# Summary merges and factors with a PSUM operand, and a new order table

## The chip, the cores and the metric

The kernel runs on one core of a Trainium2 chip. The metric is the device time of one execution in microseconds (us). Three executions of the kernel before took 1714.06, 1714.22 and 1714.65 us; the median is 1714.22 us.

## The reference

Two stages follow each other. In the first, 32 inducing vectors `I` (32 x 128) attend to a batch `x` of 12480 rows of 128 values, for each of four batches, which gives a summary `h` of 32 x 128; then every row of `x` attends to that summary. In the second, all 49920 rows go through a two-layer network with a piecewise activation.

```python
def mab(q, kv):
    s = scale * (q @ kv.transpose(0, 2, 1))
    s = s - s.max(-1, keepdims=True)
    a = np.exp(s)
    a /= a.sum(-1, keepdims=True) + 1e-09
    return a @ kv
h = mab(I, x)
attn = mab(x, h)
...
h = x @ w_in
g = np.where(h >= 1, h, np.where(h <= -1, 0.0, (h + 1) ** 2 / 4))
out = g @ w_out
```

## The kernel before

The 12480 rows of a batch are cut into 25 chunks (20 of 512 rows, 5 of 448; `SIZES`), and the chunks into seven groups (`GROUPS`: six of four chunks, the last with one). Three kinds of work are interleaved on all engines:

- **The network (`chunk`, from line 1482 on).** A chunk takes eight steps `k` over the 2048 hidden columns, two halves of 128 each. TensorE (PE) makes the hidden values into two PSUM banks (`hidden`, L1530). ScalarE (ACT) writes `relu(0.5 h + 0.5)` to the buffer `w` (`rise`, L1538) and squares it (L1524). VectorE (DVE) combines `max(h, 1)` from the bank with `w` (`bound`, L1543). For six of the eight steps `w` is then split into a rounded part `hi` (L1573 on DVE, L1571 on ACT or L1567 on GpSimd, POOL) and the rest `lo = w - hi`, which is always POOL's (L1578). PE multiplies by the second weights into an accumulator bank (`project`, L1606). At a chunk's end DVE transposes the accumulator (`oT`, L1618) and SyncE (SP) stores it. `rise` and `bound` take both halves in one instruction ("wide", 128x1024 or 128x2x448) where the order says so and the two banks lie beside each other, otherwise one half each.
- **The summary (`summarize`).** For each group, scores, their maximum, exponentials (`e`, with their sums in a column of `sg`), and the weighted sum of the rows, which `keep` (L1174) puts into `hs[:, g, :]` (128 x 128). A chain of small steps `c1` to `c13` joins the groups when the maxima of the first six are there. `c6` makes the six factors `fe` (ACT, L1221). `c7` makes `fs = fe * sg` and sums it to `early` (DVE, L1224 and L1225). `merge(g)` adds `hs[g] * fe[g]` into `he`, one group after the other (DVE, L1229 for the first, L1231 for the other five). `c8` makes `fall` (ACT, L1234), `c9` makes `tot = early * fall + sg` (DVE, L1237), `c10` folds it on PE (L1240). `c11` makes `rs` and its reciprocal and from them two scaled copies `ff` of the 128 x 32 matrix `fold` (DVE, L1243 to L1246). `c12` multiplies `he` and the last `hs` by `ff` (PE, L1250), and `c13` copies the result to `hT` (DVE, L1254). Everything that reads the next batch's summary waits for `hT`: `multiply` and the loads of `hw`, and the scores of `attend`. Batch 0's summary stands at the start, where no network work runs; those of batches 1 to 3 are interleaved with the network work of the batch before.
- **The attention (`attend`)** of each group against `hT`, with its rows sent to the buffers `aT` by DMA.

Every step is added to a `Plan` with an engine, two costs and its needs. `ORDER` gives each step its rank on its engine, `ON` picks the engine where a step has a choice, and `Plan.order` walks these lists and gives out banks and buffers. An engine works strictly in its order. The plan treats a step marked `alone` on DVE as one that can't run beside POOL. PSUM has eight banks, seven of them (`h=7`) for hidden values, scores and the chain, one (`o=1`) for the accumulator. Each of `s_m`, `s_b`, `s_t`, `s_h` in the chain holds one of the seven for a while. PE runs small products (`keep_on`, L1634) at the start where it would else be idle.

```python
def merge(g):
    if g == 0:
        nc.vector.tensor_scalar(he, hs[:, 0, :], fe[:, :1], None, op0=ALU.mult)
        return
    nc.vector.scalar_tensor_tensor(he, hs[:, g, :], fe[:, g : g + 1], he, op0=ALU.mult, op1=ALU.add)
```

Of the kernel before, what the change touches and what calls it, by code (L numbers as in the profile page):

```python
# [13 lines left out]
ALU = mybir.AluOpType  # L14
# [718 lines left out]
def attn_moe(  # L733
# [276 lines left out]
    def summarize(b):  # L1010
# [184 lines left out]
        tot = small("tot", [P, 1], f"_{b}")  # L1195
        rs = small("rs", [P, 1], f"_{b}")
        ff = small("ff", [P, 2, M], "")
        s_m, s_b, s_t, s_h = (Slot("h") for _ in range(4))

        def c1():  # L1200
            nc.vector.tensor_reduce(m1, mg[:, : NG - 1], axis=AX.X, op=ALU.max)
# [488 lines left out]
```

## Time and profile before

| what | value |
|---|---|
| median of three executions | 1714.22 us |
| the profiled execution, its own time | 1713.46 us |
| its span, first to last instruction | 1711.7 us |
| PE busy | 1683.9 us, 98% |
| DVE busy | 1640.0 us, 96% |
| ACT busy | 1648.2 us, 96% |
| POOL busy | 1610.4 us, 94% |
| mean granted TensorE clock | 0.999 |
| DMA | 105.65 MB, 62 GB/s |

A group of the profile is one line's instructions on one engine, with busy time, mean duration, and the idle time of the engine just before them with what ended it. An instruction that is held up after it has been issued shows this as a longer duration, not as idle time. Matmuls overlap, so PE's busy time is more than its work.

### The profile page before, as it was taken

Reading aid. Unit: us, or ns where it says so; the run is one execution under the profiler, and the core shown is the slowest. Engines: PE = TensorE matmul, PEld = TensorE weight load, DVE = VectorE, ACT = ScalarE, POOL = GpSimd, SP = SyncE. Lnnn points to the kernel's source line nnn. Section 1 sums busy time; section 2 is a strip of 40 time slices with the busy share of each in tenths; the row PEclk is TensorE's granted clock in tenths of the full one; section 3 lists DMA queues with packets and bytes.
Section 4 is the critical chain, followed back from the end, with each engine's and each line's share of the span. In section 5 each row is a group of like instructions: output and inputs, shape, how many; then the busy total and the mean of one; then the engine's idle time right before and its main releaser. Section 6 shows DMA issues by size and latency. Waiting matters only on the chain.

```text
span 1711.7 us, 24841 instructions
## 1 busy us (share of the span) xinstructions
PE 1683.9 (98%) x7713; PEld 1188.8 (69%) x7713; DVE 1640.0 (96%) x2040; ACT 1648.2 (96%) x2220; POOL 1610.4 (94%) x849
## 2 busy tenths in 40 slices
PE   9999999999999999999999999999999999999998
PEld 7766766767667666766766676677667766666677
DVE  7899999999999999999999999999999999999997
ACT  5999999999899999999999999999989999999997
POOL 2799999999899999999899999999989999999998
PEclk9999999999999999999999999999999999999999
DMA  6542323322333241432152432422213112011111
GB/s 250 134 92 41 81 60 68 70 48 54 76 67 70 55 86 39 80 58 56 29 108 52 85 71 49 85 50 41 42 24 66 27 31 42 19 37 42 26 32 26
DMA packets 426212, 105.65 MB, mean 62 GB/s; under 512 B 369744, under 2 KB 409776, under 8 KB 426080
## 3 DMA queue, kind: packets, MB, share of 16 engines
q1 hardware_dynamic: 424960, 103.74, 28.3%
q8 instruction: 61, 1.00, 0.2%
q14 instruction: 71, 0.58, 0.1%
q10 hardware_dynamic: 1120, 0.33, 0.1%
HBM read 48.94 MB, written 25.56 MB: 44 GB/s over the span
## 4 chain that ended last, share of the span: by engine, by line
PE 86%; DVE 7%; ACT 2%; issue 2%; DMA 1%; SPq 1%; POOL 0%; DVEq 0%; ACTq 0%; POOLq 0%
PE banks L1606 61%; PE banks L1530 19%; DVE w L1543 3%; PE banks L1167 1%; PE banks L1338 1%; PE banks L1098 1%; DVE hi L1573 1%; ACT w L1524 1%; ACT w L1538 1%; DVE oT L1618 1%; PE banks L1634 1%; PE banks L1044 1%; PE banks L1148 1%; DMA xr<-in_x 1%; DVE he L1231 0%
## 5 line engine op out<-in xcount | busy, mean ns | idle before, releaser
L1578 POOL TENSOR_TENSOR lo<-w,hi 128x1024 fp32r<-128x1024 f32 (+1 forms) x597 | 1388.3, 2355 | 41.7 <-PE banks L1606 16.3
L1543 DVE SCALAR_TENSOR_TENSOR w<-banks,w 128x1024 f32<-128x1024 f32 (+3 forms) x1098 | 950.8, 902 | 22.4 <-ACT w L1524 15.7
L1538 ACT ACTIVATE w<-banks 128x512 f32<-128x512 f32 (+3 forms) x1162 | 815.9, 753 | 22.6 <-PE banks L1530 17.1
L1524 ACT ACTIVATE w<-w 128x1024 f32<-128x1024 f32 (+1 forms) x800 | 819.5, 1052 | 5.8
L1530 PE MATMUL banks<-aT,hw 128*128 128x512 f32 (+1 forms) x1600 | 601.7, 432 | 12.4 <-DVE w L1543 10.0
L1606 PE MATMUL banks<-hi,w_lo 128*128 128x512 f32 (+1 forms) x1194 | 507.1, 425 | 4.1 <-DVE oT L1618 3.1
L1573 DVE TENSOR_REDUCE hi<-w 128x1024 fp32r<-128x1024 f32 (+1 forms) x391 | 459.5, 1180 | 11.5 <-PE banks L1606 2.9
L1606 PE MATMUL banks<-hi,w_hi 128*128 128x512 f32 (+1 forms) x1194 | 462.3, 387 | 0.0
L1606 PE MATMUL banks<-lo,w_hi 128*128 128x512 f32 (+1 forms) x1194 | 457.1, 430 | 1.9 <-DVE oT L1618 1.3
L1530 PEld LDWEIGHTS banks<-aT,hw 128*128 128x128 f32 x1600 | 296.7, 188 | 165.4 <-DVE w L1543 58.6
L1606 PE MATMUL banks<-w,w_f 128*128 128x512 f32 (+1 forms) x812 | 404.0, 582 | 0.1
L1606 PEld LDWEIGHTS banks<-hi,w_lo 128*128 128x128 f32 x1194 | 224.9, 188 | 103.2 <-issue 43.8
L1606 PEld LDWEIGHTS banks<-lo,w_hi 128*128 128x128 f32 x1194 | 223.6, 188 | 101.4 <-issue 54.3
L1606 PEld LDWEIGHTS banks<-hi,w_hi 128*128 128x128 f32 x1194 | 224.9, 188 | 59.4 <-issue 22.0
L1606 PEld LDWEIGHTS banks<-w,w_f 128*128 128x128 f32 x812 | 151.8, 188 | 38.7 <-issue 10.6
L1567 POOL TENSOR_SCALAR hi<-w 128x1024 fp32r<-128x1024 f32 (+1 forms) x140 | 144.6, 1035 | 8.4 <-DVE w L1543 5.1
L1618 DVE STREAM_TRANSPOSE oT<-banks 128x512 f32<-128x512 f32 (+1 forms) x100 | 69.8, 698 | 10.7 <-PE banks L1606 8.6
L1571 ACT CAST hi<-w 128x1024 fp32r<-128x1024 f32 (+1 forms) x66 | 67.7, 1026 | 0.5 <-DVE w L1543 0.4
L1074 DVE STREAM_TRANSPOSE xT<-xr 128x512 f32<-128x512 f32 (+1 forms) x75 | 51.3, 684 | 4.8 <-DMA xr<-in_x 4.1
L1381 POOL TENSOR_TENSOR a<-a,ahi 128x512 fp32r<-128x512 f32 (+3 forms) x28 | 35.3, 1260 | 0.0
L1370 POOL TENSOR_TENSOR s<-s,sm 128x512 f32<-128x512 f32 (+3 forms) x28 | 28.8, 1030 | 1.3 <-DVE sm L1367 0.8
L1098 PE MATMUL banks<-xT,indT 128*32 128x512 f32 (+1 forms) x224 | 29.0, 589 | 0.0
(130 smaller groups left out, 532.8 us busy)
## 6 DMA issues: line engine op xcount, KB each, us to landing
out<-oT SPq DMA_DIRECT2D x320, 64.0 KB, 2.1
xn<-in_x SPq DMA_DIRECT2D x64, 256.0 KB, 3.3
xr<-in_x SPq DMA_DIRECT2D x240, 64.0 KB, 2.5
aT<-ahi SPq DMA_DIRECT2D x158, 64.0 KB, 2.0
aT<-a SPq DMA_DIRECT2D x158, 64.0 KB, 2.0
xn<-in_x SPq DMA_DIRECT2D x20, 224.0 KB, 3.1
out<-oT SPq DMA_DIRECT2D x78, 56.0 KB, 1.9
xr<-in_x SPq DMA_DIRECT2D x60, 56.0 KB, 2.2
```

The source lines that it names most:

```text
L1074: nc.vector.transpose(make(xT[b, c])[:, : CW[c]], xr.tile[:, : NB[c]].rearrange("c n i -> c (n i)"))
L1098: nc.tensor.matmul(p[q * M : (q + 1) * M, :cw], indT, xT[b, c].tile[:, :cw], start=True, stop=True)
L1524: nc.scalar.activation(v, v, AF.Square)
L1530: nc.tensor.matmul(make(h)[:, :cw], hw[b][ft // 4].tile[:, ft % 4 * P : (ft % 4 + 1) * P], aT[b, c].tile[:, :cw], start=True, stop=True,)
L1538: each(of, i, hs_, lambda h, to: nc.scalar.activation(to, h, AF.Relu, bias=0.5, scale=0.5), cw, w)
L1543: lambda h, t: nc.vector.scalar_tensor_tensor(t, h, 1.0, t, op0=ALU.max, op1=ALU.min), cw, w,
L1567: nc.gpsimd.tensor_scalar(make(hi)[:, :, :cw], w.tile[:, :, :cw], 1.0, 0.0, op0=ALU.mult, op1=ALU.add)
L1571: nc.scalar.copy(make(hi)[:, :, :cw], w.tile[:, :, :cw])
L1573: nc.vector.tensor_reduce(make(hi)[:, :, :cw], w.tile[:, :, :cw].unsqueeze(3), axis=AX.X, op=ALU.max)
L1578: nc.gpsimd.tensor_sub(make(lo)[:, :, :cw], w.tile[:, :, :cw], hi.tile[:, :, :cw].bitcast(F32))
L1606: nc.tensor.matmul(acc.tile[:, :cw], wt[k][:, i, :], g.tile[:, i, :cw], start=first, stop=(acc.parts == 0),)
L1618: nc.vector.transpose(make(oT)[:, :nb].rearrange("c n i -> c (n i)"), acc.tile[:, :cw])
```

## The change

In the four summaries, one more PSUM bank `s_e` is taken from `c6` to the last merge. `c6` writes the factors twice, into columns 128 to 133 of that bank and to `fe`. `c7` reads the copy in the bank. The first merge goes to ACT and writes to the bank; four merges read and write the bank, the last reads the bank and writes `he` to SBUF. `c9` goes from DVE to ACT. In `c11` the reciprocal is written to the bank of `s_t`, and both `ff` read it there as a broadcast operand. `merge` is no longer marked `alone`, and some costs of the plan change. All of `ORDER` is new (of the table two lines stand here), and 28 of the 705 letters of `ON`, which decide engines.

```diff
 ORDER = [
-    0, 0, 2, 0, 4, 0, 2, -2, -2, -2, -2, -2, -2, -2, -2, -2, -2, -2, -2, -2, -2, -2, -2, -2,
+    0, 2, 0, 0, 4, 6, 6, -2, -2, -2, -2, -2, -2, -2, -2, -2, -2, -2, -2, -2, -2, -2, -2, -2,
...
-        s_m, s_b, s_t, s_h = (Slot("h") for _ in range(4))
+        s_m, s_b, s_e, s_t, s_h = (Slot("h") for _ in range(5))
...
         def c6():
-            nc.scalar.activation(fe, mg[:, : NG - 1], AF.Exp, bias=nm, scale=SCALE)
+            for p in (make(s_e)[:, C : C + NG - 1], fe):
+                nc.scalar.activation(p, mg[:, : NG - 1], AF.Exp, bias=nm, scale=SCALE)
 
         def c7():
-            nc.vector.tensor_mul(fs, fe, sg[:, : NG - 1])
+            nc.vector.tensor_mul(fs, s_e.tile[:, C : C + NG - 1], sg[:, : NG - 1])
             nc.vector.tensor_reduce(early, fs, axis=AX.X, op=ALU.add)
 
         def merge(g):
             if g == 0:
-                nc.vector.tensor_scalar(he, hs[:, 0, :], fe[:, :1], None, op0=ALU.mult)
+                nc.scalar.mul(s_e.tile[:, :C], hs[:, 0, :], fe[:, :1])
                 return
-            nc.vector.scalar_tensor_tensor(he, hs[:, g, :], fe[:, g : g + 1], he, op0=ALU.mult, op1=ALU.add)
+            nc.vector.scalar_tensor_tensor(
+                he if g == NG - 2 else s_e.tile[:, :C], hs[:, g, :], fe[:, g : g + 1], s_e.tile[:, :C],
+                op0=ALU.mult, op1=ALU.add,
+            )
...
         def c9():
-            nc.vector.scalar_tensor_tensor(tot, early, fall, sg[:, NG - 1 :], op0=ALU.mult, op1=ALU.add)
+            nc.scalar.activation(tot, early, AF.Identity, bias=sg[:, NG - 1 :], scale=fall)
...
         def c11():
             nc.vector.tensor_scalar(rs, s_t.tile[:, :1], 1e-9, None, op0=ALU.add)
-            nc.vector.reciprocal(rs, rs)
-            nc.vector.tensor_scalar(ff[:, 0, :], fold[:, 0, :], fall, rs, op0=ALU.mult, op1=ALU.mult)
-            nc.vector.tensor_scalar(ff[:, 1, :], fold[:, 0, :], rs, None, op0=ALU.mult)
+            nc.vector.reciprocal(s_t.tile[:, 1:2], rs)
+            r = s_t.tile[:, 1:2].to_broadcast([P, M])
+            nc.vector.scalar_tensor_tensor(ff[:, 0, :], r, fall, fold[:, 0, :], op0=ALU.mult, op1=ALU.mult)
+            nc.vector.tensor_mul(ff[:, 1, :], r, fold[:, 0, :])
...
-                factors = add("ACT", 100, 250, c6, [o])
+                factors = add("ACT", 200, 350, c6, [o], [s_e])
...
-        e = add("DVE", 220, 350, c7, [factors, *summed[:-1]])
+        e = add("DVE", 220, 350, c7, [factors, *summed[:-1]], [s_e])
         for g in range(NG - 1):
-            o = add("DVE", 190, 320, lambda g=g: merge(g), [o if g else state.get("chain"), factors, lasts[g]], alone=g > 0)
+            o = add(
+                "DVE" if g else "ACT", 240 if g else 170, 370 if g else 310, lambda g=g: merge(g),
+                [o if g else state.get("chain"), factors, lasts[g]], [s_e],
+            )
...
-        o = add("DVE", 90, 220, c9, [o, e, summed[-1]])
+        o = add("ACT", 100, 250, c9, [o, e, summed[-1]])
         o = add("PE", 120, 300, c10, [o], [s_t])
-        o = add("DVE", 420, 560, c11, [o, fell, state.get("chain")], [s_t])
+        o = add("DVE", 440, 580, c11, [o, fell, state.get("chain")], [s_t])
```

The order of the instructions moves as follows at the summary of batch 1; batches 2 and 3 look alike. On DVE before, at the end of the chain (`tot` is `c9`; `w` and `hi` are the network's; line numbers are those of the kernel before):

```order
L1237 SCALAR_TENSOR_TENSOR tot_134<-early_132,fall_133,sg 128x1
L1618 STREAM_TRANSPOSE oT_4368<-banks 128x448
L1243 TENSOR_SCALAR rs_135<-banks 128x1
L1244 RECIPROCAL rs_135<-rs_135 128x1
L1245 TENSOR_SCALAR ff<-fold,fall_133,rs_135 128x32
L1246 TENSOR_SCALAR ff<-fold,rs_135 128x32
L1543 SCALAR_TENSOR_TENSOR w_4335<-banks,w_4335 128x448
```

On DVE now, the rows that lead up to the same point (line numbers are eight higher there for the network's lines):

```order
L1232 SCALAR_TENSOR_TENSOR banks<-hs,fe_130,banks 128x128
L1551 SCALAR_TENSOR_TENSOR w_4249<-banks,w_4249 128x448
L1232 SCALAR_TENSOR_TENSOR banks<-hs,fe_130,banks 128x128
L1225 TENSOR_TENSOR fs_131<-banks,sg 128x6
L1226 TENSOR_REDUCE early_132<-fs_131 128x1
L1232 SCALAR_TENSOR_TENSOR banks<-hs,fe_130,banks 128x128
L1551 SCALAR_TENSOR_TENSOR w_4257<-banks,w_4257 128x2x448
L1232 SCALAR_TENSOR_TENSOR banks<-hs,fe_130,banks 128x128
L1551 SCALAR_TENSOR_TENSOR w_4276<-banks,w_4276 128x448
L1232 SCALAR_TENSOR_TENSOR he<-hs,fe_130,banks 128x128
L1626 STREAM_TRANSPOSE oT_4326<-banks 128x448
L1247 TENSOR_SCALAR rs_135<-banks 128x1
```

Before, the six merges of batch 1 stood up to 64 rows ahead of `rs` (rows 432 to 468 of DVE's order, `rs` being row 496); now the five that DVE keeps stand in rows 485 to 494, `rs` being row 496 again. On ACT before, at the same place (`fall` is `c8`):

```order
L1538 ACTIVATE w_4335<-banks 128x2x448
L1123 ACTIVATE e_1171_4342,sg<-banks,nb_6_143 32x448
L1234 ACTIVATE fall_133<-mb_128,nb_6_143 128x1
L1524 ACTIVATE w_4335<-w_4335 128x2x448
L1538 ACTIVATE w_4358<-banks 128x2x448
```

On ACT now:

```order
L1222 ACTIVATE banks<-mg,nm_127 128x6
L1222 ACTIVATE fe_130<-mg,nm_127 128x6
L1546 ACTIVATE w_4276<-banks 128x448
L1230 ACTIVATE banks<-hs,fe_130 128x128
L1238 ACTIVATE fall_133<-mb_128,nb_6_143 128x1
L1532 ACTIVATE w_4257<-w_4257 128x2x448
L1546 ACTIVATE w_4276<-banks 128x448
L1123 ACTIVATE e_1172_4296,sg<-banks,nb_6_143 32x448
L1532 ACTIVATE w_4276<-w_4276 128x2x448
L1241 ACTIVATE tot_134<-early_132,sg,fall_133 128x1
```

The factors, which stood 66 rows ahead of `fall`, now stand four rows ahead of it, and the first merge and `tot` have come in between the network's instructions. Over the whole program, 53 more of ACT's `rise` and 52 more of DVE's `bound` are wide (`rise` of 128x1024: 402 against 349; `bound` of 128x1024: 444 against 404, of 128x2x448: 110 against 98).

## Rows read from the trace of the kernel before

**Rows 1.** Page, parts 1 and 2: busy time by engine; POOL in 40 slices.

```profile
PE 1683.9 (98%) x7713; PEld 1188.8 (69%) x7713; DVE 1640.0 (96%) x2040; ACT 1648.2 (96%) x2220; POOL 1610.4 (94%) x849
...
POOL 2799999999899999999899999999989999999998
```

**Rows 2.** PE, PEld, DVE, ACT, POOL busy (instructions), clock, DMA, GB/s: stretch without summary.

```profile
1498.00:1620.00 122.00, 121.70 (x466) 84.36 (x466) 119.37 (x135) 121.61 (x153) 121.01 (x60) 1.00 0.17 36
```

**Rows 3.** Groups by line and shape: the changed instructions (busy us, mean ns | idle before).

```profile
L1231 DVE SCALAR_TENSOR_TENSOR he<-hs,fe,he 128x128 f32<-128x128 f32 x20 | 13.7, 685 | 0.1
...
L1237 DVE SCALAR_TENSOR_TENSOR tot<-early,fall,sg 128x1 f32<-128x1 f32 x4 | 4.0, 995 | 0.0
L1246 DVE TENSOR_SCALAR ff<-fold,rs 128x32 f32<-128x32 f32 x4 | 3.9, 971 | 0.0
...
L1229 DVE TENSOR_SCALAR he<-hs,fe 128x128 f32<-128x128 f32 x4 | 2.8, 703 | 0.0
...
L1224 DVE TENSOR_TENSOR fs<-fe,sg 128x6 f32<-128x6 f32 x4 | 2.6, 656 | 0.0
...
L1245 DVE TENSOR_SCALAR ff<-fold,fall,rs 128x32 f32<-128x32 f32 x4 | 2.4, 612 | 0.1
```

**Rows 4.** Two lines' instructions: duration ns min/median/max, first and last start.

```profile
L1231 DVE SCALAR_TENSOR_TENSOR he<-hs,fe,he x20: 322/350/2634, 32.7 to 1272.3; 128x128 f32<-128x128 f32 x20
L1246 DVE TENSOR_SCALAR ff<-fold,rs x4: 227/235/3187, 36.4 to 1270.4; 128x32 f32<-128x32 f32 x4
```

**Rows 5.** Timelines of DVE, POOL and PE around 430 us: start, us, what.

```profile
430.55 3.19 DVE L1246 TENSOR_SCALAR ff<-fold,rs 128x32 f32<-128x32 f32 x1
...
431.64 2.06 POOL L1578 TENSOR_TENSOR lo<-w,hi 128x896 fp32r<-128x896 f32 x1
...
434.32 0.97 PE L1530 MATMUL banks<-aT,hw 128*128 128x448 f32 x2 [2.94 <-DVE w L1543]
```

**Rows 6.** Busy time in short stretches around the changed instructions, columns as in rows 2.

```profile
428.00:436.00 8.00, 4.72 (x22) 3.51 (x21) 7.77 (x12) 4.03 (x8) 5.70 (x4) 0.91 0.26 49
...
806.00:815.00 9.00, 8.07 (x37) 5.08 (x36) 8.93 (x14) 8.16 (x14) 8.93 (x4) 1.00 0.20 35
844.00:856.00 12.00, 10.41 (x52) 8.00 (x52) 11.76 (x19) 10.05 (x19) 8.95 (x5) 1.00 0.24 58
...
1208.00:1222.00 14.00, 12.89 (x56) 8.06 (x54) 13.49 (x20) 13.14 (x19) 12.72 (x8) 1.00 0.17 32
1236.00:1250.00 14.00, 11.78 (x51) 8.85 (x50) 13.96 (x15) 11.02 (x17) 11.11 (x8) 1.00 0.15 33
1262.00:1280.00 18.00, 15.63 (x81) 10.86 (x83) 17.69 (x28) 14.53 (x28) 15.67 (x10) 1.00 0.07 14
```

**Rows 7.** The same columns, just behind the stall at 430 us.

```profile
434.00:436.00 2.00, 1.68 (x5) 1.54 (x6) 2.00 (x5) 0.98 (x3) 0.00 (x0) 0.63 0.55 104
436.00:438.00 2.00, 2.00 (x7) 1.78 (x6) 0.90 (x2) 1.68 (x2) 1.04 (x1) 0.52 0.17 39
```

**Rows 8.** Groups by line and shape: instructions that price what is added.

```profile
L1543 DVE SCALAR_TENSOR_TENSOR w<-banks,w 128x1024 f32<-128x1024 f32 x404 | 483.3, 1212 | 10.1 <-ACT w L1524 8.7 <-POOL lo L1578 0.2 <-issue 0.2
...
L1538 ACT ACTIVATE w<-banks 128x1024 f32<-128x1024 f32 x349 | 355.9, 1030 | 3.4 <-PE banks L1530 1.4 <-POOL lo L1578 0.8 <-issue 0.2
...
L1538 ACT ACTIVATE w<-banks 128x512 f32<-128x512 f32 x582 | 329.2, 612 | 3.6 <-PE banks L1530 1.9 <-POOL s L1370 0.7
L1543 DVE SCALAR_TENSOR_TENSOR w<-banks,w 128x512 f32<-128x512 f32 x472 | 302.1, 677 | 7.2 <-ACT w L1524 4.1 <-issue 1.4
...
L1074 DVE STREAM_TRANSPOSE xT<-xr 128x512 f32<-128x512 f32 x60 | 41.8, 697 | 4.4 <-DMA xr<-in_x 4.1 <-issue 0.2
...
L1174 ACT COPY hs<-banks 128x128 f32<-128x128 f32 x24 | 6.5, 276 | 2.3 <-PE banks L1167 2.3
...
L1353 DVE TENSOR_TENSOR s<-banks,mx 128x512 f32<-128x512 f32 x19 | 12.8, 674 | 0.0
...
L1105 DVE TENSOR_SCALAR nb<-ml,mb 128x1 f32<-128x1 f32 x4 | 0.9, 214 | 0.1
```

More of the change, by code (lines that the diff above doesn't have):

```diff
@@ L43 @@
     -2, -2, -2, -2, -2, -2, -2, -2, -2, -2, -2, -2, -2, -2, -2, -2, -2, -2, -2, -2, -2, -2, -2, -2,
[492 rows of a table removed]
[492 rows of a table added]
 ]
 ON = (
-    "DPPDDDDDDDDAADDAADAADDDAADADAAAADAADADAASSSASSASSSSSSSASPPAPPPAPPPPPDAADDDDADDADADAAAAAAADAAPAPAAAAD"
-    "AAPAPDPPDAADPPDDDPADDPDDDDPDDADDPDDDADDDPPDDAPDDDDDDPDPDDDDAPDDDPDAPPDDPDPDDDPDDPDDDADDDPDADPPDDDDPD"
-    "DDPDDDPAADDDDDADPDDPDPDPDPDADDPADPADPPPPDADDDADDADDPDDDPDADDPDPDDPDADDDDDADPDPPDPADDDPDDDDPDDDAPPDDA"
-    "DDDPDADDDDPDPDDDDADDDPDPDPPDADDDPDDDDPDDDADPDPDAPDADDDPDDDPDDDDDPDPDADAPDDPDDADDDPDDDDPDAPPPADDPDDDA"
-    "ADDAADDAPDPDADPPDDDDDDDDPDDDDPDDADPDPDDPDDPDDDPDPDADDDAPPDDADDPPDDDPDDDDDDDPDPADADPDDDADDDDPDDDPDDAD"
-    "PPADPDPDDDDDDDPDDDPDPDAPDDDADDPDPDDDDPDDPPDDDPADDDDADDPDPDPDDDPDDDDDPDDDPDDDDDPDADADDDDPDDDDDDPDDDDP"
+    "DPPDDDPDDDDAADDAADDADDAAADADAAAAAAADADAASSSASSASSSSSSSASPPAPPAAPPPPPPAADDDDADDADADAAAAAAADAAPAPAAAAD"
+    "AAPAPDPDDADAPPDPDPDDDPDDDDPDDADDPDDDADDDPPDDAPDDDDDDPDPDDDDAPDDDPDAPPDDPDPDDDPDDPDDDADDDPDADPPDDDDPD"
+    "DDPDDDPAADDDDDADDDDPDPDPDPAPDDPADPADPPPPDADDDADDADDPDDDPDADDPDPDDPDADDDDDADPDPPDPADDDPDDDDPDDDAPPDDA"
+    "DDDPDADDDDPDPDDDDADDDPDPDPPDADDDPDDDDPDDDADPDPDAPDADDDPDDDPDDDDDPDPDADADDDPDDADDDPPPDDDPAPPPADDPDDDA"
+    "ADDAAADAPDPDADPPDDDDDDDDPDDDDPDDADPDPDDPDDPDDDPDPDADDDAPPDDADDPPDDDPDDDDDDDPDPADADPDDDADDDDPDDDPDDAD"
+    "PPADPDPDDDDDDDPPDDPDDDAPDADDDDDPPDDDDPDDPDPDDPADDDDADDPDPDPDDDPDDDDDPDDDPDDDDDPDADADDDDPDDDDDDPDDDDP"
     "DDDDADADPDDDDADDDPDDPDDDADDDPDDDDDDPADDDDDDPPDDDADDDPDDDDPDDDDPDDDADDDPDDDDPDDADADDPDDDDPADDDDDPDDDD"
```

984 rows, old and new, of the table ORDER are left out of this document.

## The prediction

> **What bounds the kernel now.** I read the page first. PE is busy for 98% of the span, ACT and DVE for 96% each, POOL for 94%, and POOL is at nine tenths almost everywhere behind the first slices [rows 1]. So no engine has much to give, and time can only be won where one makes the others wait. The stretches come next. In a stretch behind the last summary, PE is without work for 0.30 us of 122 us, or 0.25% [rows 2]; there is nothing to win there. Around the chains it is different. I looked up where the changed instructions stand and asked for the busy times around them: six short stretches of 75 us together, in which PE is busy for 63.5 us [rows 6]. It is idle for 3.28, 0.93, 1.59, 1.11, 2.22 and 2.37 us, 11.5 us in all, while DVE is busy for 7.77 of 8 us and 13.96 of 14 us in the worst of them. PE waits there for DVE.
>
> What DVE does in this time is in the durations. A merge takes 322 ns at least and 350 ns in the median, but up to 2634 ns, and the second `ff` takes 227 ns or 3187 ns for the same 32 columns [rows 4]. The timeline shows what ends the long one: `ff` starts at 430.55 us, and its 3.19 us end at 433.74 us, as POOL's `lo`, begun at 431.64 us and 2.06 us long, ends at 433.70 us. PE then resumes after 2.94 us of idle time that DVE's next `bound` ended [rows 5]. So an instruction of DVE with all its operands in SBUF stands still until POOL's instruction is through. [...]
>
> **What the change takes off DVE.** The rows of network instructions price an operand in PSUM: `bound` takes 677 ns for 512 columns and 1212 ns for 1024 [rows 8], hence 1.045 ns a column and 142 ns fixed, and a 128-column merge would take 276 ns, a 32-column `ff` 175 ns, `fs` 150 ns. Against the busy times of [rows 3]: the 20 merges fall from 13.7 to 5.5 us (8.2 less), the four first merges leave DVE (2.8), as does `tot` (4.0), the two kinds of `ff` fall by 3.2 and 1.7, and `fs` by 2.0. The sum is 21.9 us less of DVE.
>
> [...]
>
> **What it adds.** ACT gets three instructions in each of four summaries, the second factors, the first merge and `tot`. A copy of 128 x 128 on ACT takes 276 ns [rows 8], so 12 x 0.28 = 3.4 us. Against that, 53 more `rise` are wide, each saving 2 x 612 - 1030 = 194 ns, 10.3 us; and 52 more `bound`, each 2 x 677 - 1212 = 142 ns, 7.4 us [rows 8]. I cost both at nothing: PE's 99.75% in the quiet stretch covers them [rows 2], and without that cover ACT could give back 6.9 us and DVE 7.4 us at the most.
>
> Two new waits are on the path. The first of DVE's merges now waits for ACT's, and PE's fold waits for `tot` in ACT's queue, where in the new order one to three `rise` stand ahead of it. No row of before shows such a wait. It costs nothing if the `bound` rows that stand between the merges cover it, and two wide `rise` (2 x 1.03 us) in each of three batches if nothing does, 6.2 us. I take one half `rise`, 0.6 us, for each batch, as the order puts half ones there: 1.8 us. Behind the waiting instructions stand `bound` and `oT`, on which PE's next banks and accumulator depend.
>
> Batch 0's chain runs while POOL has little to do (2 tenths in the first slice [rows 1]), and its merges are near the shortest already; I count it as nothing, with 0.5 us to either side. The few preparations of weights that change engine lie there too and go to engines with room.
>
> The order table moves everything else by a little, SP's queue included. What such moves can do is seen in the loads: DVE waits 4.1 us in all for `xr` before its transposes [rows 8]. All of that may vanish or as much come anew, so I take 0 and keep 4 us for the range.
>
> **The sum.** I let the path gain what PE loses in the six stretches: 11.5 us less the 0.2 us that 0.25% of 75 us would be anyway, and the 1.7 us of the clock, 13.0 us. Against it stand 1.8 us of new waits. The profiled execution took 1713.46 us, 1.8 us over its span, so the change should bring it to 1702.3 us. It lay 0.8 us under the median of the runs, 1714.22 us, and by the median I predict **1703.0 us**. Once the waits for POOL are gone, late next is ACT with its squares and `rise`, which is almost as full as PE [rows 2].
>
> **The rivals.**
> *Only the great stall is worth something.* The stall at 430 us is the one place where PE is idle for half of a stretch [rows 6]. In the others ACT may be the next to be late, since DVE is hardly shorter of time than it. Then only 3.3 + 1.7 us come back and 1.8 go: 1711.0 us. Against it speaks that PE idles in all six stretches, each time less than DVE's instructions are prolonged. Chance 0.15, about half of it within the bound of no change.
>
> *All of DVE's time was on the path.* Then 21.9 us come back less 1.8: 1694.1 us. For it, DVE is busy for nearly the whole of the six stretches; against it, PE lost only 11.5 us there. Chance 0.10.
>
> *The change does not do what it says.* `hs` and the factor `fe` still come from SBUF, and if two such reads are enough for the wait, it stays, and only the new waits are added: 1716.0 us, still within no change. Against it, `s`, with a bank and `mx` from SBUF, takes 674 ns for 512 columns in the mean of 19, no more than `bound`, and `nb`, with its scalar `mb` from SBUF, 214 ns in the mean of four, though POOL is nearly always at work [rows 8]. [...] Chance 0.07.
>
> *The bank costs more than the waits did: slower.* `s_e` takes one of seven banks from the factors to the last merge, while `s_t` and the last scores want banks as well. If PE then lacks a neighbouring pair, each pair of hidden values waits for one more wide `bound`, 1.21 us [rows 8]. With five pairs in each of three batches that is 18.2 us, and 1703.0 + 18.2 = 1721.2 us. It decides for slower from twelve such waits on (11.2 + 3.4 over 1.21). For it, PE's first wait in the long idle of [rows 5] is of this kind. Against it, the new order holds the bank for only some ten rows of DVE and has more wide instructions, which need neighbours, not fewer. Chance 0.13.
>
> **How the numbers follow.** The forecast itself has 0.55, with 1698 to 1708 us as its own range: the 4 us of the loads and some of the new waits. A measurement of this kernel can tell about 0.2%, 3.4 us, from no change. Faster by more than that are the forecast, the rival with all of DVE's time and half of the first: 0.72. Within it are the other half and the change that does not act: 0.15. Slower is the bank: 0.13. The range from 1694 to 1714 us holds the forecast and the first two rivals, 0.80.
>
> **What will show it.** In the changed profile no merge, `ff` or `fs` may take over 400 ns, and DVE's busy time should be some 29 us less (21.9 + 7.4). PE should be idle for under 1 us in each stretch around the merges of batches 1 to 3, and the granted clock stay whole. If ACT's first merge or `tot` stands in the chain with DVE idle ahead of the next instruction, the new waits are larger than taken. Long merges would mean that the wait stayed; PE idle until `bound`, with short merges, that the bank was missed. I am wrong if the waits go and the time stays over 1711 us, or if PE's idle time turns up elsewhere, at loads or stores that the new order put too late.

## The result and the profile after

The changed kernel takes 1695.83 us in the median of four runs (1694.89 to 1697.46), the kernel before 1714.24 us: a ratio of 0.9893 with a 95% interval of 0.9876 to 0.9910, or 18.4 us less. The profiled execution took 1694.89 us, with a span of 1693.1 us. The forecast was 1703.0 us with 1694 to 1714 us as the range: the direction and the place were right, the size was not. The time lies 2 us under the 1698 to 1708 us that the forecast gave for itself; the wide range holds it only because it took in the rivals.

The page's first part, to be held against [rows 1]:

```profile
PE 1677.6 (99%) x7711; PEld 1187.0 (70%) x7711; DVE 1614.7 (95%) x1976; ACT 1644.2 (97%) x2181; POOL 1611.9 (95%) x851
```

DVE is busy for 25.3 us less, ACT for 4.0 us less, POOL for as long as before. What became of DVE's changed instructions is in the groups by line and shape (after):

```profile
L1232 DVE SCALAR_TENSOR_TENSOR banks<-hs,fe,banks 128x128 f32<-128x128 f32 x16 | 5.5, 346 | 0.0
L1230 ACT ACTIVATE banks<-hs,fe 128x128 f32<-128x128 f32 x4 | 1.6, 396 | 0.0
L1241 ACT ACTIVATE tot<-early,sg,fall 128x1 f32<-128x1 f32 x4 | 1.5, 377 | 0.0
...
L1232 DVE SCALAR_TENSOR_TENSOR he<-hs,fe,banks 128x128 f32<-128x128 f32 x4 | 1.3, 330 | 0.0
...
L1250 DVE SCALAR_TENSOR_TENSOR ff<-banks,fall,fold 128x32 f32<-128x32 f32 x4 | 1.0, 250 | 0.2
L1251 DVE TENSOR_TENSOR ff<-banks,fold 128x32 f32<-128x32 f32 x4 | 0.7, 180 | 0.0
...
L1225 DVE TENSOR_TENSOR fs<-banks,sg 128x6 f32<-128x6 f32 x4 | 0.7, 164 | 0.7 <-ACT banks L1230 0.6
```

They take 9.2 us together, against 29.4 us in [rows 3], and no merge is long any more: in the view of [rows 4], those that write to the bank have

```profile
L1232 DVE SCALAR_TENSOR_TENSOR banks<-hs,fe,banks x16: 317/346/356, 33.8 to 1254.6; 128x128 f32<-128x128 f32 x16
```

Where the span's 18.6 us went is read best by cutting both traces at two instructions that stand at the same progress of the network in both orders: `m` (L1201, the start of a chain's maximum) and `hT` (L1254, in the new kernel L1259, its end). The columns are those of [rows 2]. Before, the three chains among network work, and the stretch behind the last:

```profile
373.33:441.31 67.98, 64.18 (x309) 48.12 (x308) 63.85 (x95) 61.67 (x92) 60.11 (x32) 0.97 0.18 42
...
804.32:862.88 58.56, 56.05 (x285) 41.95 (x284) 56.75 (x81) 55.22 (x84) 52.20 (x29) 1.00 0.25 55
...
1206.08:1279.16 73.08, 67.38 (x320) 48.31 (x319) 71.22 (x93) 64.87 (x99) 64.07 (x36) 1.00 0.16 30
1279.16:1711.70 432.54, 424.38 (x1692) 302.03 (x1691) 416.51 (x487) 421.36 (x549) 415.78 (x209) 1.00 0.17 35
```

After, the same:

```profile
373.00:435.91 62.91, 62.91 (x313) 47.39 (x312) 59.48 (x87) 62.34 (x90) 61.58 (x34) 1.00 0.25 55
...
798.82:853.45 54.63, 54.63 (x280) 41.20 (x279) 51.73 (x80) 54.42 (x86) 53.08 (x30) 1.00 0.28 61
...
1196.54:1262.24 65.70, 65.70 (x321) 48.69 (x320) 62.48 (x88) 64.61 (x96) 63.16 (x35) 1.00 0.15 29
1262.24:1693.10 430.86, 423.92 (x1692) 302.14 (x1691) 415.16 (x478) 420.20 (x548) 417.14 (x210) 1.00 0.17 35
```

The three chains are shorter by 5.07, 3.93 and 7.38 us, 16.4 us in all, and PE is busy for the whole of each. The stretches between them, 363.01 and 343.20 us before (441.31 to 804.32 and 862.88 to 1206.08 us), are 362.91 and 343.09 us long now (435.91 to 798.82 and 853.45 to 1196.54 us), the same within 0.1 us each; the first 373 us give 0.3 us and the last stretch 1.7 us. So a table of numbers that was changed from end to end moved hardly anything where no chain runs. Inside the three chains its wide `bound` saved nothing either: that line keeps DVE busy for 104.2 us of them before and 104.9 us after.

### The profile page after: what moved, and what is told of

It is laid out like the page before. It is cut to its first block, busy times and chain, and to the rows that moved or that the text cites. A ratio compares the mean times of both kernels' runs of the same rounds, so it can differ in the third digit from the quotient of the medians.

```text
span 1693.1 us, 24692 instructions
## 1 busy us (share of the span) xinstructions
PE 1677.6 (99%) x7711; PEld 1187.0 (70%) x7711; DVE 1614.7 (95%) x1976; ACT 1644.2 (97%) x2181; POOL 1611.9 (95%) x851
## 4 chain that ended last, share of the span: by engine, by line
PE 85%; DVE 5%; ACT 3%; issue 2%; DMA 2%; POOL 1%; SPq 1%; DVEq 0%; ACTq 0%; POOLq 0%
PE banks L1614 61%; PE banks L1538 19%; DVE w L1551 2%; ACT w L1546 1%; DVE hi L1581 1%; PE banks L1167 1%; PE banks L1346 1%; PE banks L1098 1%; ACT w L1532 1%; POOL lo L1586 1%; DVE oT L1626 1%; PE banks L1148 1%; DMA w<-in_moe_w_in 0%; DMA xr<-in_x 0%; DMA lo<-in_x 0%
## 5 line engine op out<-in xcount | busy, mean ns | idle before, releaser
L1551 DVE SCALAR_TENSOR_TENSOR w<-banks,w 128x512 f32<-128x512 f32 (+3 forms) x1046 | 946.9, 938 | 26.1 <-ACT w L1532 18.0
L1538 PE MATMUL banks<-aT,hw 128*128 128x512 f32 (+1 forms) x1600 | 592.8, 429 | 3.0 <-DVE w L1551 1.9
```

What stands on the lines that cost most here:

```text
L1538: nc.tensor.matmul(make(h)[:, :cw], hw[b][ft // 4].tile[:, ft % 4 * P : (ft % 4 + 1) * P], aT[b, c].tile[:, :cw], start=True, stop=True,)
L1551: lambda h, t: nc.vector.scalar_tensor_tensor(t, h, 1.0, t, op0=ALU.max, op1=ALU.min), cw, w,
```

## The experiments

Three theories stood against each other. W: DVE lost its waits for POOL because its changed instructions no longer take all their tensors from SBUF. O: the new order with its wide instructions made the difference. A: it was the first merge and `tot`, which went to ACT. The kernel before ran beside them: 1714.69 us in the median beside the first four kernels, 1714.95 us beside the last three.

**New order, old operands.** The changed kernel with its order and engines, but with `fs`, merges and `ff` as they were:

```diff
-            nc.vector.tensor_mul(fs, s_e.tile[:, C : C + NG - 1], sg[:, : NG - 1])
+            nc.vector.tensor_mul(fs, fe, sg[:, : NG - 1])
...
-                nc.scalar.mul(s_e.tile[:, :C], hs[:, 0, :], fe[:, :1])
+                nc.scalar.mul(he, hs[:, 0, :], fe[:, :1])
...
+            nc.vector.scalar_tensor_tensor(he, hs[:, g, :], fe[:, g : g + 1], he, op0=ALU.mult, op1=ALU.add)
...
+            nc.vector.reciprocal(rs, rs)
+            nc.vector.tensor_scalar(ff[:, 0, :], fold[:, 0, :], fall, rs, op0=ALU.mult, op1=ALU.mult)
+            nc.vector.tensor_scalar(ff[:, 1, :], fold[:, 0, :], rs, None, op0=ALU.mult)
```

> The new order table and the new engines (first merge and tot on ACT), but fs, the merges, the reciprocal and both ff read and write SBUF alone again. If the gain comes from DVE no longer waiting for POOL (theory W), the waits return, now in a cluster in each of batches 1 to 3: of the 20 us that DVE's changed instructions lost, 10 to 18 us come back, 1706 to 1714 us, with single merges or ff of 1 to 3 us. If it comes from the new order and its wide instructions (theory O), the time stays under 1699 us. If it comes from the two instructions that went to ACT (theory A), it also stays under 1699 us.

1712.3 us (1710.31 to 1713.63), 0.9985 of before (0.9976 to 0.9994). The waits are back, by groups:

```profile
L1232 DVE SCALAR_TENSOR_TENSOR he<-hs,fe,he 128x128 f32<-128x128 f32 x20 | 18.0, 902 | 0.2
...
L1225 DVE TENSOR_TENSOR fs<-fe,sg 128x6 f32<-128x6 f32 x4 | 3.2, 809 | 0.2 <-ACT fe L1222 0.2
...
L1246 DVE TENSOR_SCALAR ff<-fold,fall,rs 128x32 f32<-128x32 f32 x4 | 1.2, 301 | 0.2
...
L1247 DVE TENSOR_SCALAR ff<-fold,rs 128x32 f32<-128x32 f32 x4 | 0.9, 236 | 0.0
```

DVE's instructions take 23.3 us against 9.2 us. The two `ff` are short here (301 and 236 ns), and POOL ran nothing beside them in any of the chains: the merges ahead of them had waited POOL's instructions out, and POOL's next one came later. In batch 1 POOL's `lo` ended at 433.24 us, the two `ff` ran from 434.23 to 434.67 us, and POOL's next instruction began at 435.49 us. Two short stretches, at the chains of batches 1 and 2, show what comes on top, in the columns of [rows 2]:

```profile
430.00:438.00 8.00, 6.68 (x24) 5.55 (x25) 7.74 (x13) 4.49 (x6) 5.40 (x4) 0.57 0.20 39
850.00:858.00 8.00, 7.19 (x23) 6.32 (x23) 7.56 (x17) 5.72 (x9) 2.04 (x2) 0.57 0.43 101
```

PE is granted 0.57 of its clock in both, after PE had stood still: for 1.98 us ahead of 429.99 us, until `bound`, and at the second place for 2.68 us, until ACT's `eN`, and 0.81 us, until `bound`. That is 0.43 x 8 = 3.4 us of clock at each place, at most, since PE was idle for 1.3 and 0.8 us of them; the kernel before lost 1.7 us at one place [rows 7]. O and A find no support: the new order and ACT's share are all there, and 2.4 us of the gain is left. By itself this run doesn't exclude that the order is worth more, since the waits, now close together, cost more of the clock than before (up to 3.4 us at each of two places against 1.7 us at one); the next one does.

**Old order, no waits.** The kernel before with stand-ins of the same shape:

```diff
-            nc.vector.tensor_mul(fs, fe, sg[:, : NG - 1])
+            nc.vector.tensor_reduce(fs, fe.unsqueeze(2), axis=AX.X, op=ALU.max)
...
-            nc.vector.scalar_tensor_tensor(he, hs[:, g, :], fe[:, g : g + 1], he, op0=ALU.mult, op1=ALU.add)
+            nc.vector.tensor_reduce(he, hs[:, g, :].unsqueeze(2), axis=AX.X, op=ALU.max)
...
-            nc.vector.scalar_tensor_tensor(tot, early, fall, sg[:, NG - 1 :], op0=ALU.mult, op1=ALU.add)
+            nc.vector.tensor_scalar(tot, early, fall, sg[:, NG - 1 :], op0=ALU.mult, op1=ALU.add)
...
-            nc.vector.tensor_scalar(ff[:, 1, :], fold[:, 0, :], rs, None, op0=ALU.mult)
+            nc.vector.tensor_reduce(ff[:, 1, :], fold[:, 0, :].unsqueeze(2), axis=AX.X, op=ALU.max)
```

> The old order table and engines, all in SBUF, but each waiting instruction of DVE is replaced by one of the same shape with a single tensor input of a kind that is not held up: fs, the merges and both ff are reductions over an axis of one (they leave out the factors, the sums of the merges and the scaling of ff), tot takes fall and the last sum as scalars. W: DVE loses its waits without any new order, so 1694 to 1700 us, with PE idle for under 3 us in the six stretches. O and A: nothing of the new order or of ACT's share is in it, so 1712 to 1716 us.

1695.96 us (1695.38 to 1696.43), 0.9893 of before (0.9878 to 0.9908): the whole gain, the same ratio as the change, with the order table of before, all of it in SBUF, and nothing more on ACT. The stand-ins take 9.7 us of DVE with `tot` and the first merge, the changed instructions 9.2 us, so they don't win by being cheaper. By the groups by line and shape a reduction of `hs` takes 276 ns:

```profile
L1231 DVE TENSOR_REDUCE he<-hs 128x128 f32<-128x128 f32 x20 | 5.5, 276 | 0.1
```

And by the busy times in two stretches (columns of [rows 2]) PE is not idle at the place of the great stall nor at that of batch 3:

```profile
428.00:436.00 8.00, 8.00 (x46) 6.44 (x45) 7.46 (x16) 7.82 (x13) 7.56 (x6) 1.00 0.27 51
...
1245.00:1265.00 20.00, 20.00 (x108) 13.80 (x107) 18.90 (x34) 19.18 (x33) 19.24 (x12) 1.00 0.10 18
```

From `m` to `hT`, as above, its three chains are 182.3 us long together, against 199.6 us before and 183.2 us in the changed kernel, and PE is idle for 0.02 us of them:

```profile
373.63:435.49 61.86, 61.84 (x309) 46.94 (x308) 58.65 (x95) 61.34 (x92) 60.00 (x33) 1.00 0.19 43
797.97:853.17 55.20, 55.20 (x285) 42.44 (x284) 52.52 (x82) 54.60 (x84) 52.25 (x29) 1.00 0.25 56
1195.82:1261.01 65.19, 65.19 (x320) 48.96 (x319) 61.79 (x93) 64.10 (x99) 63.07 (x36) 1.00 0.17 34
```

**One part at a time in the new order.** First only the merges in SBUF:

> The changed kernel with only the merges in SBUF again (the first on ACT still); fs and ff keep the bank. W: the merges' share of the waits, about a third before (6.8 of some 20 us), returns: 1700 to 1706 us. O and A: under 1698 us.

1710.69 us (1709.94 to 1711.5), 0.9978 of before (0.9968 to 0.9987), more than W had expected. The merges alone take

```profile
L1232 DVE SCALAR_TENSOR_TENSOR he<-hs,fe,he 128x128 f32<-128x128 f32 x20 | 19.4, 972 | 0.4 <-ACT he L1230 0.2
```

12.6 us more than in the bank (6.8 us). The expectation had carried over their share from the old order, where they were spread over 30 to 56 us. Close together they wait more often: of the 15 of DVE's merges in batches 1 to 3 that have two tensors, 12 take over 400 ns here and 6 did before. Why that is so no run takes apart. Then only the reciprocal and `ff` in SBUF:

> The changed kernel with only the reciprocal and both ff in SBUF again. W: the two ff lost about 4.5 us before, 3.6 us of it at one place; with three batches and a wait of 1 to 2 us in each, 1698 to 1702 us. O and A: under 1698 us.

1702.42 us (1700.87 to 1704.89), 0.9932 (0.9917 to 0.9947), 0.4 us over W's span:

```profile
L1249 DVE TENSOR_SCALAR ff<-fold,fall,rs 128x32 f32<-128x32 f32 x4 | 5.3, 1313 | 0.2
L1250 DVE TENSOR_SCALAR ff<-fold,rs 128x32 f32<-128x32 f32 x4 | 2.8, 706 | 0.0
```

8.1 us against 1.7 us for the two, and 6.6 us more time. The two prices against the changed kernel, 14.9 and 6.6 us, add up to more than the 16.5 us of both at once: with the merges in SBUF as well, the `ff` met no instruction of POOL and took 301 and 236 ns, as shown above.

**One part at a time in the old order.** The merges as reductions, all else as before:

> The old order and engines; only the six merges are replaced by reductions of the same shape (they leave out the factors and the sums of the merges), while fs, tot and ff stay as they were. Theory W, by DVE's time: the merges and the first merge of batches 1 to 3 were prolonged by about 8.5 us in the trace of before (20 merges at 685 against 346 ns, and the first ones), so at nine tenths of that on the path, 1706 to 1709 us. By PE's idle time, as the prediction took it, their share is about 5 us: 1709 to 1711 us. Theory O: 1714 us.

1707.49 us (1705.95 to 1713.36), 0.9956 (0.9944 to 0.9968), or 7.5 us less, within W's span by DVE's time; one of the eight runs took 1713.36 us, the others 1709.26 us at most. And, with the merges as before, `ff` from the bank and `tot` with one tensor input:

```diff
-            nc.vector.scalar_tensor_tensor(tot, early, fall, sg[:, NG - 1 :], op0=ALU.mult, op1=ALU.add)
+            nc.vector.tensor_scalar(tot, early, fall, sg[:, NG - 1 :], op0=ALU.mult, op1=ALU.add)
...
-            nc.vector.reciprocal(rs, rs)
-            nc.vector.tensor_scalar(ff[:, 0, :], fold[:, 0, :], fall, rs, op0=ALU.mult, op1=ALU.mult)
-            nc.vector.tensor_scalar(ff[:, 1, :], fold[:, 0, :], rs, None, op0=ALU.mult)
+            nc.vector.reciprocal(s_t.tile[:, 1:2], rs)
+            r = s_t.tile[:, 1:2].to_broadcast([P, M])
+            nc.vector.scalar_tensor_tensor(ff[:, 0, :], r, fall, fold[:, 0, :], op0=ALU.mult, op1=ALU.mult)
+            nc.vector.tensor_mul(ff[:, 1, :], r, fold[:, 0, :])
```

> The old order and engines; only the reciprocal and ff use the bank of s_t as in the change, and tot takes fall and the last sum as two scalars, with one tensor input. The merges and fs stay in SBUF. It computes the reference. Theory W, by DVE's time: ff lost 4.6 us and tot 3.1 us in batches 1 to 3, and the stall at 430 us lost 1.7 us of the clock besides: 1705 to 1709 us if that is all on the path. If only the great stall counts: 1709 to 1711 us. Theory O: 1714 us.

1704.59 us (1704.03 to 1705.8), 0.9939 (0.9924 to 0.9953), or 10.4 us less, without a new table and without another bank, and 0.4 us under W's span:

```profile
L1231 DVE SCALAR_TENSOR_TENSOR he<-hs,fe,he 128x128 f32<-128x128 f32 x20 | 13.8, 690 | 0.1
...
L1237 DVE TENSOR_SCALAR tot<-early,fall,sg 128x1 f32<-128x1 f32 x4 | 1.0, 262 | 0.0
...
L1246 DVE SCALAR_TENSOR_TENSOR ff<-banks,fall,fold 128x32 f32<-128x32 f32 x4 | 1.0, 251 | 0.1
```

The two parts give 17.9 us of the 18.7 us that the run without any wait gave. The part with the great stall is the larger one although it freed less of DVE: 7.6 us (the busy times of `tot` and both `ff` in [rows 3], 10.3 us, less 2.7 us now) against 9.9 us for the merges. It also gave back the clock, which is 1.00 in all three chains there. With only the merges free, the stall behind `ff` stayed, and in the profiled execution the clock lost some 5 us in two chains, where the kernel before lost 1.7 us:

```profile
373.46:441.19 67.73, 64.42 (x308) 48.50 (x308) 62.72 (x95) 61.54 (x92) 60.03 (x32) 0.95 0.18 42
805.07:864.25 59.18, 56.98 (x285) 43.45 (x284) 56.37 (x81) 54.74 (x84) 52.17 (x29) 0.97 0.25 55
```

**Read or write?** The new order, merges with two tensors read from SBUF but written to the bank:

```diff
             nc.vector.scalar_tensor_tensor(
-                he if g == NG - 2 else s_e.tile[:, :C], hs[:, g, :], fe[:, g : g + 1], s_e.tile[:, :C],
+                he if g == NG - 2 else s_e.tile[:, :C], hs[:, g, :], fe[:, g : g + 1], he,
                 op0=ALU.mult, op1=ALU.add,
```

> The new order; the merges read two tensors in SBUF as in the run with all merges in SBUF, but write to the bank, all but the last (they leave out the running sum). If the second read from SBUF is what is held up, the merges wait as there: 1708 to 1712 us, mean merge about 900 ns. If the write to SBUF counts too, the time lies near the changed kernel: 1696 to 1700 us.

1711.49 us (1707.65 to 1713.62), 0.9978 (0.9968 to 0.9987), as with all merges in SBUF:

```profile
L1232 DVE SCALAR_TENSOR_TENSOR banks<-hs,fe,he 128x128 f32<-128x128 f32 x16 | 14.4, 900 | 0.3 <-ACT he L1230 0.3
```

So for a merge that reads two tensors from SBUF it was of no account where it wrote (900 ns in the mean to the bank, 902 and 972 ns to SBUF in the two runs above), and two such reads were enough for the wait. The last merge of the changed kernel says the same from the other side: it writes `he` to SBUF, reads the bank, and takes 330 ns.

**Is it POOL that holds them?** No run takes POOL's work away, but the traces of all these kernels show where the waits end. In the kernel before and in the six runs that have such waits, 71 of the chains' DVE instructions (lines of `c7` to `c11`) take over 400 ns. Every one ends just behind the end of an instruction of POOL: merges 133 to 161 ns behind, the first merge of the old order 83 to 88, `ff` 36 to 43, `fs` and `tot` 10 to 28. None of them belongs to batch 0, where POOL runs little (8.8 of the first 43 us before). Two merges beside POOL's `lo`, the first from the run with the old operands in the new order, the second from the changed kernel:

```profile
431.49 1.90 DVE L1232 SCALAR_TENSOR_TENSOR he<-hs,fe,he 128x128 f32<-128x128 f32 x1
431.15 2.09 POOL L1582 TENSOR_TENSOR lo<-w,hi 128x896 fp32r<-128x896 f32 x1 [0.27 <-PE banks L1610]
...
841.36 0.34 DVE L1232 SCALAR_TENSOR_TENSOR banks<-hs,fe,banks 128x128 f32<-128x128 f32 x1
841.26 4.20 POOL L1586 TENSOR_TENSOR lo<-w,hi 128x896 fp32r<-128x896 f32 x2
```

The first starts 0.34 us behind POOL's instruction and ends 0.15 us behind its end. The second runs in the midst of POOL's work and is not held; so do 13 of the 15 merges of batches 1 to 3 in the changed kernel, and all 15 take 300 to 356 ns.

Not tried: holding the bank for longer, to price it, and the new operands with the old table, where the bank would be held for 31 to 60 us (from `fe` to the last merge before). What 53 wide instructions more are worth was not taken out alone either. The stretches without chains are the same within 0.1 us, so there the new table as a whole is worth nothing.

## Why the prediction was right, and where its size was off

*The mechanism* was as read: DVE's instructions with operands in SBUF stood still for POOL (the second `ff` for up to 3187 ns), and PE for DVE (2.94 us, until the `bound` behind that `ff`). With the new order and the waits 2.4 us of the gain is left, with the old order and without the waits all of it is there. The reading was too wide in one point: "an instruction of DVE with all its operands in SBUF stands still" does not hold for each. In the trace of before, `early` (159 ns, L1225) and the reciprocal of `rs` (164 ns, L1244), from SBUF to SBUF, run beside POOL's instructions and are not held. The step "no merge, `ff` or `fs` over 400 ns" came true, and the granted clock is whole (1.00) in all three chains.

*What DVE gives up.* 21.9 us were reckoned, 20.2 us came (29.4 less 9.2). The durations were a little short: a merge from the bank takes 346 ns, not the 276 ns that the slope of `bound` gave; an `ff` 250 and 180 ns, not 175. All told DVE is busy for 25.3 us less, where some 29 were reckoned; wide `bound` saved 3.9 us (its line's busy time went from 950.8 to 946.9 us), not 7.4. Beside the shortest merge from SBUF before, 322 ns, a merge of 276 ns would have been the cheaper one; with 346 ns measured it is not, and the last section compares merges that ran without POOL beside them.

*What of it the path gains* is the term that was mis-sized. "I let the path gain what PE loses in the six stretches" put 13.0 us there, 1.7 us of them for the clock (0.37 x 2 + 0.48 x 2 us, by its shares of 0.63 and 0.52 in [rows 7]), and the three chains gave 16.4 us. The failing step was to read the loss from PE's idle time. In the chains before, PE was idle for 3.80, 2.51 and 5.70 us, 12.0 us, and the clock took 1.7 us; the missing 2.7 us are in its busy time, which fell from 187.6 to 183.2 us, 4.4 us with the clock's, for as many matmul records (914). Matmuls overlap in the records (before, at 429.4 us, those of 448 columns are 0.36 to 0.37 us long and start 0.20 to 0.21 us apart), so I take it that a PE that gets its next one a little late still shows as busy; no run takes this apart. DVE's busy time was the better measure: in these three stretches it fell by 18.1 us, and the path by nine tenths of that. Of the rivals, the one that put all of DVE's time on the path, 1694.1 us, came nearest; it had 0.10. That it is within 2 us is in part luck: DVE gave up less than it reckoned and nine tenths of that reached the path, but the new waits that it subtracted did not come.

*The new waits* were taken at 1.8 us and are not there: PE is idle for 0.0 us in all three chains. Elsewhere ACT's first merge ended DVE's idle time once, for 0.6 us (the row of `fs` above), and `tot` that of PE once, for 0.6 us, both in batch 0's chain. The three instructions on ACT cost 1.6 + 1.5 + 1.2 us, 4.3 us for 3.4 us reckoned, and hide, as was said.

*The other rivals.* That only the great stall counts is refuted: the chains of batches 2 and 3, which have none such, gave 11.3 us. That the factor, still read from SBUF, keeps the wait alive is refuted by the 346 ns beside POOL, with the factor, a scalar, and one tensor in SBUF. That the bank costs more than the waits did is refuted as well: PE is not idle in the chains.

*The order.* It was taken at 0 with 4 us to either side, and came to some 2 us, 1.7 us of them behind the last chain. That is one execution against one, and the four runs of the changed kernel lie 2.6 us apart; by the medians, the old table without waits is 0.1 us from the new kernel. What the new table is for is not shown by a run. I take it to make room for the bank: it puts the merges so close together that `s_e` is held for some 5 us in batch 1 (423.7 to 428.8 us).

## What to carry to other kernels

Where GpSimd is busy nearly all the time (94% here), look at the durations of VectorE's small instructions, minimum against maximum: one that takes many times its shortest time can be waiting inside its record, as the merges were here (2634 against 322 ns), and no idle time shows it (0.1 us ahead of all 20). Look then for what ends at the same moment on GpSimd (10 to 161 ns earlier here). Take one of its tensors from PSUM (a merge then took 346 ns), or choose a form with one tensor input that isn't held up (`tot` as a `tensor_scalar`, 262 ns), and do it in the order as it stands before searching for a new one; `tot` and the two `ff` alone, with no further bank, gave 10.4 us here, where the whole change gave 18.4. To size such a wait, count the time that the held engine loses, and add the clock that TensorE loses behind a long stall (1.7 us before); TensorE's own idle time was too little here (12.0 us against 16.4).

## What was not expected of the hardware

- The prediction counted tensors and places; the form counts too. A `tensor_scalar` with one tensor in SBUF waited for POOL (`ff`, 128 x 32, up to 3187 ns before, 1313 ns in the mean in the run that put it back), while a `tensor_reduce` of the same shape, from SBUF to SBUF, did not (177 ns in the mean and less in the old order, six of the eight beside POOL; the 20 of a merge's shape 276 ns). Nor did a `tensor_scalar` on one column with two scalars from SBUF (`tot`, 262 ns in the mean of four, three of them beside POOL); whether it is the scalars or the single column that spares it, no run shows.
- PSUM made a merge neither dearer nor, as was reckoned, cheaper. In batch 0, where POOL ran nothing beside them, five merges took 346 to 350 ns with both tensors in SBUF and 339 to 350 ns with one in PSUM.
- A long stall can cost once more in the clock: with the operands put back, PE had 0.57 of its clock for 8 us at two places, up to 3.4 us at each, behind stalls of 2.0 us and of 2.7 and 0.8 us. It need not: in the chain of batch 3 of the kernel before PE was idle for 5.70 us in all, for 1.42 us at the longest, and the clock was 1.00.
